# A three-stage attention kernel: its order of work taken from the framework's scheduler and written by a list schedule of its own

## The chip, the cores and the metric

The kernel runs on one core of a Trainium2 chip. The metric is the device time of one execution in microseconds. The core has a matmul engine (TensorE, PE in the rows, its weight loads PEld), VectorE (DVE), ScalarE (ACT), GpSimd (POOL), and SP, which only issues transfers here. Each engine works through its own instructions in order; the engines wait for each other by semaphores.

## The reference

Three stages follow each other on 4 batches of 544 positions (32 global and 512 local; 8 heads of 64, so 512 columns).

- Phase A, local and global attention: a local query sees the keys at a distance of at most 32 and the 32 global keys; a global query sees all 544. Softmax, then times v.
- Phase B, four experts of one head each: `logits = x @ w_gate`, the top two of four are kept with softmax weights; per expert `q = x @ wq[e]`, `k = x @ wk[e]`, `v = x @ wv[e]`, causal softmax attention, and `a @ v @ wo[e]`, summed with the gate weights.
- Phase C: `h = relu(x @ w_in)`, a convolution of three taps along the sequence, `h * sigmoid(conv) @ w_out`.

w_in, w_out and conv_w come as 64-bit floats, the others as 32-bit.

## The kernel before, in words

Work goes batch by batch through the phases; phase A takes a batch in four pairs of heads (16 pairs in all). Matmuls with accuracy to keep take each operand as a high and a low half (`split`, `sub`: L93 to L101) and issue three products for one.

A pair of phase A loads keys and queries (`raw`, L230, two buffers) and values (`vr`, L236, two buffers of 1 MB), makes the scores of the global queries (L244) and of the local ones (L261 adds the mask, L266 the scores), reduces to the maximum (L272), takes eight exps with their sums (L275), scales on POOL (L281), transposes (L296), and multiplies with v (L307; L320 for global queries) into `xh`, `xl`, of which there are five buffers (L217).

Phase B of a batch projects q and k (L378, 8 groups of 12 matmuls) and v with the gate (L391), computes the gate on VectorE, handles the last 32 rows apart (L438 and on), and goes through eight items (`scores`, `trans`, `pv`): score matmuls (L476), maximum, exp (L483) into two `w2` buffers, scaling on POOL (L490), transposes (L500), copies into two more `w2` buffers (L502), and times v (L512) into `oh`, `ol`. There are six `w2` buffers (L67); transfers of weights and the outputs take them too.

Phase C of a batch has two halves z. For each of eight f: six matmuls (L558), relu (L565 or L568), the middle tap (L570), two further taps on VectorE (L578, twice), tanh (L581), gating (L585), and a split into `gh`, `gl` (eight buffers each). `project` then runs through four m with 24 matmuls each (L598) and sends the result out (L603).

Two jobs are done once. The fold (`fold_gen`, L174) multiplies wo into w_in (L193), using `oh`, `ol` for its operand, so the first batch's `pv` comes after it. `wout_gen` (L208) prepares w_out. Both take 16 tiles of 64-bit floats through `load64` and `decode` (L103 to L116), six VectorE instructions and one of ScalarE, and one subtraction on POOL (L91).

The order is set in two steps. Three generators (phase A; projections and phase B; fold, w_out and phase C) yield estimated times, and `merge` (L628) takes the next piece from the one whose clock is lowest, at rates 60, 46 and 36, with flags for what must wait. That gives the program order. The framework's scheduler then orders each engine's instructions, with program order as priority and a timing model of its own; only groups in `paired()` keep their order on TensorE.

Of the kernel before, what the change touches and what calls it, by code (L numbers as in the profile page):

```python
# [8 lines left out]
F32 = mybir.dt.float32  # L9
# [24 lines left out]

def local_mask():

    import numpy as np
    m = np.zeros((128, 4, 128), np.float32)
    q = np.arange(32)[:, None]
    for n in range(NG_):  # L40
        for c, kb in enumerate(KEYS[FIRST[n]:FIRST[n] + 4]):
            if kb != "g":
                t = 32 * kb + np.arange(32)[None, :]
                ok = (abs(q + 32 * n - t) <= 32) & (t >= 0) & (t < SL)
                m[32 * (n % 4):32 * (n % 4) + 32, n // 4, 32 * c:32 * c + 32] = np.where(ok, 0.0, -BIG)
    return m


@with_exitstack
def body(ctx, tc, kq, vA, w_gate, wqk, wv, woT, w_in, conv_w, w_out, cmask, out):  # L50
    nc = tc.nc
    NB = kq.shape[0]
    pe, act, dve, pool, sp = nc.tensor, nc.scalar, nc.vector, nc.gpsimd, nc.sync
# [4 lines left out]
    def T(shape, dt, name, bufs=1):  # L58
        return sb.tile(shape, dt, name=name, bufs=bufs)

    def PS(*shape):
        return ps.tile([128] + list(shape), F32, name="s", bufs=5)

    def PO(*shape):
        return ps.tile([128] + list(shape), F32, name="t", bufs=3)

    NW = 6  # L67
# [14 lines left out]

    def paired():

        return tc.manual_schedule(engines={mybir.EngineType.PE})
# [17 lines left out]
    def decode(raw, w, dst=None):  # L103

        lo, up = raw[:, :, 0], raw[:, :, 1]
        t, f1, p, q = W1("hb", I32)[:, :w], W1("cv", I32)[:, :w], W1("hb", I32)[:, :w], W1("cv")[:, :w]
        dve.tensor_scalar(t, up, 3, 0x3FFFFFF8, op0=ALU.logical_shift_left, op1=ALU.bitwise_and)
        dve.scalar_tensor_tensor(f1, up, -0x40000000, t, op0=ALU.bitwise_and, op1=ALU.bitwise_or)
        dve.tensor_scalar(p, f1, -0x800000, None, op0=ALU.bitwise_and)
        dve.scalar_tensor_tensor(q, lo.bitcast(U32), 2.0 ** -52, p.bitcast(F32), op0=ALU.mult, op1=ALU.mult)  # L110
        dve.tensor_tensor(q, f1.bitcast(F32), q, op=ALU.add)

        e = W1("hb")[:, :w]
        act.activation(e, up.bitcast(F32), AF.Abs)
        dst = q if dst is None else dst
        dve.scalar_tensor_tensor(dst, e, GUARD, q, op0=ALU.is_ge, op1=ALU.mult)  # L116
# [9 lines left out]
    make_identity(nc, ident)  # L126
# [20 lines left out]
    flags = {"x_free": 0, "x_done": 0, "o_free": 0, "o_done": 0}  # L147

    def wait(flag, n):
        while flags[flag] < n:  # L150
            yield None

    def projections_gen():
        w = W2()
# [7 lines left out]
        for c in range(4):  # L162
            w = W2()
            sp.dma_start(w, wqk[128 * c:128 * c + 128])
            split(wqkh[:, c], wqkl[:, c], w, act)
            yield 3
        for c in range(4):
            w = W2()
# [3 lines left out]
            yield 3  # L172

    def fold_gen():  # L174

        woh = oh.rearrange("p a c -> p (a c)")[:, :1024].rearrange("p (c m) -> p c m", c=4)
        wol = ol.rearrange("p a c -> p (a c)")[:, :1024].rearrange("p (c m) -> p c m", c=4)
        for c in (0, 2):
# [3 lines left out]
        yield 1  # L182
        for n in range(4):
            accs = [PS(512) for _ in range(2)]
            for c in range(4):
                w = load64(w_in[128 * c:128 * c + 128, 256 * n:256 * n + 256])
# [3 lines left out]
                for m in range(2):  # L190
# [4 lines left out]
                yield 1.5  # L195
# [4 lines left out]
            yield 1  # L200
        flags["o_free"] = 2

    def conv_load():
        rawc = T([128, 24, 2], I32, "rawc")
# [3 lines left out]
    def wout_gen(n):  # L208
        for f in range(8):
            w = load64(w_out[128 * f:128 * f + 128, 256 * n:256 * n + 256])  # L210
# [3 lines left out]
            yield 2.5  # L214


    XB = 5  # L217
# [4 lines left out]
    Pg = T([64, 6, 128], F32, "Pg")  # L222
    pool.memset(Pg, 0.0)
# [9 lines left out]
    def load_v(n):  # L233

        vr = T([128, NG_, 128], F32, "vr", 2)
        sp.dma_start(vr, vA[n // 4, n % 4])  # L236
        return vr

    def scores_g(k, q):
# [3 lines left out]
        for z, kk in enumerate((k[:, 32:672].rearrange("p (m c) -> p m c", m=5)[:, :, 32:], k[:, 672:736])):  # L243
            pe.matmul(gt[z], q[:, SL:], kk, start=True, stop=True)  # L244
# [8 lines left out]
    def scores_l(k, q):  # L253
# [3 lines left out]
        with paired():  # L257
# [10 lines left out]
        yield 1.5  # L268
        ml = T([128, 2, 16], F32, "ml", 2)
        P = [T([128, 4, 128], F32, "Pa", 2) for _ in range(2)]  # L270
        for y in range(2):
# [5 lines left out]
            yield 0.5  # L277
# [6 lines left out]
    def trans_g():  # L284
        PGT = T([128, 6, 64], F32, "PGT")
        t = PO(6, 64)
        for m in range(6):
            pe.transpose(t[:, m, :], Pg[:, m], ident[:64, :64])
# [3 lines left out]
    def trans_l(P):  # L292
        PA = T([128, 4, 128], F32, "PA", 2)
        t = PO(4, 128)
        for i in range(4):
            pe.transpose(t[:, i, :], P[:, i], ident)  # L296
        act.activation(PA, t, AF.Copy)  # L297
        return PA

    def pv_l(vr, PA):  # L300

        o = PO(4, 128)
        with paired():
            for g in range(NG_):
                q = slice(32 * (g % 4), 32 * (g % 4) + 32)
                for y in range(2):
                    pe.matmul(o[64 * y:64 * y + 64, g // 4, q], vr[:, g, 64 * y:64 * y + 64], PA[y][:, g // 4, q],  # L307
# [3 lines left out]
    def pv_end(b, c, o, vr, PGT):  # L311
        xh, xl = xs[b, c] = T([128, S], F32R, "xh", XB), T([128, S], F32R, "xl", XB)
# [4 lines left out]
        with paired():  # L317
            for m, g in enumerate(PGW):
                for y in range(2):
                    pe.matmul(o[64 * y:64 * y + 64, :32], vr[:, g, 64 * y:64 * y + 64],  # L320
# [4 lines left out]
    def stream_a():  # L325

        NP = 4 * NB
        raw, vr = {}, {}
        for n in range(2):
            raw[n], vr[n] = load_kq(n), load_v(n)  # L330
# [3 lines left out]
        P = None  # L334
        for n in range(NP + 1):
            old, new = n >= 1, n < NP
            if old:
                PGT = trans_g()
                yield 0.3
                PA = [trans_l(P[y]) for y in range(2)]  # L340
                yield 0.9
            if new:
                scores_g(*raw[n])
                yield 0.8
            if old:
                b, c = divmod(n - 1, 4)
                yield from wait("x_free", b if c >= XB - 4 else b - 1)
                o = pv_l(vr[n - 1], PA)
                yield 1.0
            if new:  # L350
                P = yield from scores_l(*raw.pop(n))
                if n + 2 < NP:
                    raw[n + 2] = load_kq(n + 2)
            if old:
                pv_end(b, c, o, vr.pop(n - 1), PGT)
                yield 0.5
                if c == 3:
                    flags["x_done"] = b + 1
                if n + 1 < NP:
                    vr[n + 1] = load_v(n + 1)  # L360
# [3 lines left out]
    qll = T([128, 2, 128], F32R, "qlast_l")  # L364
    def phase_b(b):
        yield from wait("x_done", b + 1)
        xh, xl = zip(*[xs.pop((b, c)) for c in range(4)])
        qh, qlo, kh, kl = [T([128, 2, S], F32R, n) for n in ("qh", "qlo", "kh", "kl")]
        for t, (dh, dl, sc) in enumerate(((qh, qlo, 0.125), (kh, kl, 1.0))):
            for p in range(2):  # L370
                m = slice(256 * t + 128 * p, 256 * t + 128 * p + 128)
                for z in range(2):
# [3 lines left out]
                    for c in range(4):  # L376
# [4 lines left out]
                    yield 1.35  # L381
# [3 lines left out]
        for i in range(5):  # L385
# [3 lines left out]
            for c in range(4):  # L389
# [6 lines left out]
            yield 1.1  # L396
        flags["x_free"] = b + 1
# [26 lines left out]
        yield 0  # L424
# [8 lines left out]
        for z in range(2):  # L433
            t = PS(512)
            n = 0
            for p in range(2):
# [4 lines left out]
            if z:  # L441
# [11 lines left out]
        yield 1.5  # L453
        PLT = T([128, 5, 128], F32, "PLT")
        t = PO(4, 128)
        for j in range(4):
# [5 lines left out]
        yield 0.7  # L462
# [3 lines left out]
        def scores(p, i):  # L466
# [5 lines left out]
            with paired():  # L472
# [6 lines left out]
            PB = []  # L479
            for y in range(2):  # L480
                dve.tensor_reduce(st[:, y:y + 1], t[y][:, :w], axis=AX.X, op=ALU.max, negate=True)  # L481
                P = W2()
                act.activation(P[:, :w], t[y][:, :w], AF.Exp, bias=st[:, y:y + 1],  # L483
                               accum_out=st[:, 2 + y:3 + y])
                PB.append(P)
            yield 0.3 * (i + 1)
# [7 lines left out]
        def trans(p, i):  # L494
            PB = live[p, i]
            live[p, i] = []
            for y in range(2):
                t = PO(4, 128)
                for j in range(i + 1):
                    pe.transpose(t[:, j, :], PB[y][:, 128 * j:128 * j + 128], ident)  # L500
                PT = W2().rearrange("p (a b) -> p a b", a=4)
                dve.tensor_copy(PT[:, :i + 1], t[:, :i + 1])  # L502
                live[p, i].append(PT)
                yield 0.2 * (i + 1)

        def pv(p, i):
            PT = live.pop((p, i))
            o = PO(512)
            with paired():
# [4 lines left out]
            d = slice(128 * i, 128 * i + 128)  # L514
            act.activation(oh[:, p, d], o[:, :128], AF.Copy)
            sub(ol[:, p, d], o[:, :128], oh[:, p, d])
            yield 0.3 * (i + 1)
# [195 lines left out]
```

## Time and profile before

| what | value |
|---|---|
| median of 3 runs | 555.01 us (552.49 to 556.65) |
| the profiled execution | 555.79 us, its span 554.0 us |
| mean granted TensorE clock | 0.927 |
| PE, PEld, DVE, ACT, POOL busy | 503.8, 420.4, 356.2, 312.3, 131.7 us |
| HBM read and written | 38.66 MB and 4.46 MB |
| chain that ended last | PE 66%, DVE 17%, ACT 7%, DMA 5%, POOL 2%, issue 2% |

The span runs from the first instruction to the last. PE counts the time in which at least one matmul is running, with modelled ends; PEld that in which weights are loaded. The granted clock is the share of full speed (2.4 GHz) that TensorE was given.

### The profile page before, as it was taken

The page shows a single profiled execution, that of the slowest core. Times are in us where ns is not written, and L with a number is a line of the kernel's source. Part 1 is how long each engine was busy: PE and PEld are TensorE (multiplying, and loading weights), DVE is VectorE, ACT ScalarE, POOL GpSimd, SP SyncE. Part 2 cuts the span into 40 slices and gives each one's busy share as a digit, 9 for nine tenths or more (in the row PEclk, how much of TensorE's full clock was granted, in tenths as well). Part 3 has the DMA queues.
Part 4 walks back from the last instruction along what each step waited for, and adds up shares of the span by engine and source line. Part 5 has one row for each costly group of instructions (what it writes and reads, how often), then busy time and mean ns, then how long its engine had stood idle before and what let it go on. Part 6 is the DMA issues. An engine that isn't in the chain of part 4 may idle for free.

```text
span 554.0 us, 14597 instructions
## 1 busy us (share of the span) xinstructions
PE 503.8 (91%) x5688; PEld 420.4 (76%) x5688; DVE 356.2 (64%) x1059; ACT 312.3 (56%) x1048; POOL 131.7 (24%) x222
## 2 busy tenths in 40 slices
PE   3598798998987998999989999988999999999996
PEld 1266577995645687987667899976889998779996
DVE  1999976335557599975786429435694565694953
ACT  2657575434543567747786448246573663573764
POOL 2244452202242252224313300022221001231000
PEclk9787985997858799999999999979999999999999
DMA  8856622202324152013432200001000000000011
GB/s 336 256 156 215 224 95 102 77 1 89 128 96 147 69 173 77 1 52 109 137 123 72 83 21 1 12 20 69 11 12 32 11 2 21 10 12 11 31 41 43
DMA packets 16742, 44.06 MB, mean 80 GB/s; under 512 B 2592, under 2 KB 7840, under 8 KB 14624
## 3 DMA queue, kind: packets, MB, share of 16 engines
q1 hardware_dynamic: 16672, 43.12, 22.6%
q8 instruction: 45, 0.74, 0.6%
q14 instruction: 25, 0.20, 0.1%
HBM read 38.66 MB, written 4.46 MB: 78 GB/s over the span
## 4 chain that ended last, share of the span: by engine, by line
PE 66%; DVE 17%; ACT 7%; DMA 5%; POOL 2%; issue 2%; SPq 0%; ACTq 0%; POOLq 0%; DVEq 0%
PE s L598 18%; PE s L378 8%; PE s L558 7%; PE s L391 5%; PE t L512 3%; PE t L307 3%; ACT Pa L275 3%; PE s L476 3%; PE t L500 3%; PE s L266 3%; PE t L296 3%; DVE ml L272 2%; PE t L320 2%; DMA w<-in_woT_dram 2%; DVE cv L578 2%
## 5 line engine op out<-in xcount | busy, mean ns | idle before, releaser
L578 DVE SCALAR_TENSOR_TENSOR cv<-hb,cw,cv 128x272 f32<-128x272 f32 x128 | 65.8, 527 | 15.9 <-ACT cv L570 14.2
L598 PE MATMUL s<-gl,wuh 128*128 128x272 f32 x256 | 73.9, 296 | 0.0
L598 PE MATMUL s<-gh,wuh 128*128 128x272 f32 x256 | 71.2, 303 | 2.2 <-ACT w L483 1.9
L598 PE MATMUL s<-gh,wul 128*128 128x272 f32 x256 | 73.2, 294 | 0.0
L490 POOL TENSOR_SCALAR w<-w,stB,gate 128x128 f32<-128x128 f32 (+3 forms) x64 | 43.4, 688 | 91.3 <-DVE stB L488 64.3
L275 ACT ACTIVATE Pa<-s,ml 128x128 f32<-128x128 f32 x128 | 45.3, 376 | 15.7 <-DVE ml L273 13.9
L598 PEld LDWEIGHTS s<-gh,wuh 128*128 128x128 f32 x256 | 46.9, 193 | 4.7 <-ACT w L483 2.4
L598 PEld LDWEIGHTS s<-gl,wuh 128*128 128x128 f32 x256 | 49.2, 193 | 1.3 <-issue 1.1
L598 PEld LDWEIGHTS s<-gh,wul 128*128 128x128 f32 x256 | 48.9, 192 | 0.3
L281 POOL TENSOR_TENSOR Pa<-Pa,ml 128x512 f32<-128x512 f32 x32 | 33.6, 1070 | 39.3 <-DVE ml L279 28.5
L502 DVE COPY w<-t 128x128 f32<-128x128 f32 (+3 forms) x64 | 30.2, 485 | 19.8 <-PE t L500 19.5
L558 PE MATMUL s<-oh,wfh 128*128 128x274 f32 x128 | 39.8, 311 | 0.6 <-ACT hb L568 0.5
L378 PE MATMUL s<-xh,wqkh 128*128 128x272 f32 x128 | 38.5, 301 | 1.7 <-ACT hb L565 1.4
L307 PEld LDWEIGHTS t<-PA,vr 128*64 128x64 f32 x1024 | 35.2, 143 | 5.8 <-ACT PA L297 2.3
L307 PE MATMUL t<-PA,vr 128*64 128x32 f32 x1024 | 38.0, 228 | 1.5 <-ACT PA L297 1.5
L483 ACT ACTIVATE w<-s,stB 128x128 f32<-128x128 f32 (+3 forms) x64 | 33.4, 531 | 8.8 <-DVE stB L481 7.2
L378 PE MATMUL s<-xh,wqkl 128*128 128x272 f32 x128 | 37.7, 294 | 0.0
L378 PE MATMUL s<-xl,wqkh 128*128 128x272 f32 x128 | 37.4, 292 | 0.0
L558 PE MATMUL s<-ol,wfh 128*128 128x274 f32 x128 | 37.2, 291 | 0.0
L558 PE MATMUL s<-oh,wfl 128*128 128x274 f32 x128 | 37.2, 290 | 0.0
L581 ACT ACTIVATE cv<-cv 128x272 f32<-128x272 f32 x64 | 27.4, 429 | 12.7 <-DVE cv L578 12.4
L587 ACT ACTIVATE gh<-cv 128x272 fp32r<-128x272 f32 x64 | 27.4, 430 | 11.9 <-DVE cv L585 11.5
(158 smaller groups left out, 1357.3 us busy)
## 6 DMA issues: line engine op xcount, KB each, us to landing
vr<-in_vA_dram SPq DMA_DIRECT2D x16, 1024.0 KB, 5.1
raw<-in_kq_dram SPq DMA_DIRECT2D x16, 672.0 KB, 4.3
out_dram<-w SPq DMA_DIRECT2D x32, 136.0 KB, 1.8
w<-in_w_in_dram SPq DMA_DIRECT2D x16, 256.0 KB, 3.8
w<-in_w_out_dram SPq DMA_DIRECT2D x16, 256.0 KB, 3.3
w<-in_wqk_dram SPq DMA_DIRECT2D x4, 256.0 KB, 3.6
w<-in_woT_dram SPq DMA_DIRECT2D x2, 256.0 KB, 8.2
w<-in_wv_dram SPq DMA_DIRECT2D x4, 128.0 KB, 2.7
```

What stands on the lines that cost most here:

```text
L275: act.activation(P[y][:, i], t[y][:, i], AF.Exp, bias=ml[:, y, i:i + 1], scale=SCALE, accum_out=ml[:, y, 4 + i:5 + i])
L281: pool.tensor_tensor(P[y], P[y], ml[:, y, 12:16, None].to_broadcast([128, 4, 128]), op=ALU.mult)
L307: pe.matmul(o[64 * y:64 * y + 64, g // 4, q], vr[:, g, 64 * y:64 * y + 64], PA[y][:, g // 4, q], start=True, stop=True)
L378: pe.matmul(acc[:, :272], wa[:, c, m], xa[c][:, s], start=(n == 0), stop=(n == 11))
L391: pe.matmul(acc[:r, :260], xa[c][:, 128 * i:128 * i + r], wa[:, c, :], start=(n == 0), stop=(n == 11))
L483: act.activation(P[:, :w], t[y][:, :w], AF.Exp, bias=st[:, y:y + 1], accum_out=st[:, 2 + y:3 + y])
L490: pool.tensor_scalar(PB[y][:, :w], PB[y][:, :w], st[:, 4 + y:5 + y], gate[:, i, 2 * p + y:2 * p + y + 1], op0=ALU.mult, op1=ALU.mult)
L502: dve.tensor_copy(PT[:, :i + 1], t[:, :i + 1])
L558: pe.matmul(acc[:, :274], a[:, p, 128 * f:128 * f + 128], x[:, p, a0:a0 + 274], start=(k == 0), stop=(k == 5))
L578: dve.scalar_tensor_tensor(cv[:, :N], hb[:, o:o + N], cw[:, k, f:f + 1], cv[:, :N], op0=ALU.mult, op1=ALU.add)
L581: act.activation(cv[:, :N], cv[:, :N], AF.Tanh, scale=0.5)
L598: pe.matmul(acc[:, :N], w[:, f, sl], a, start=(f == 0 and k == 0), stop=(f == 7 and k == 2))
```

## The change

The three generators, the flags and `merge` go. All calls are recorded as nodes (an instruction, or a `group` of TensorE's that stays together), with tiles that have no memory yet; overlaps of what is read and written give the dependences. Each node has a due time, set by `due()`, and a cost by functions of the code. `schedule` runs a clock: at each event, for each engine that is free, it takes the ready node with the lowest due time whose new buffers are to be had. `engines` is in the order in which they first occur: DVE, POOL, SP, ACT, PE. A node that lacks a buffer marks that name as lacking for later nodes of the same event. Nodes that depend on nothing, all loads of weights among them, are ready from the start. `emit` writes the nodes in that order, with a manual schedule for every engine. `claim` takes a buffer for a tile at the group that precedes its first writer.

Buffers: `w2` five in place of six; `decode` has `d0`, `d1` (two each) in place of `hb`, `cv`; the transposed items have `PT` (two) and the outputs `y` (two) in place of `w2`; `xh`, `xl` four in place of five; `vr` three halves in place of two wholes, with two transfers to a pair.

The arithmetic is as before. The core of the diff:

```diff
+PERIOD, A_AT, A_STEP, LOAD_AHEAD = 60.0, 0.0, 10.0, 20.0
+B_AT, LAST, ITEMS, ITEM_STEP = 30.0, 34.0, 14.0, 2.5
+C_AT, C_HALF, C_PROJ = 75.0, 25.0, 12.0
+FOLD, FOLD_STEP, WOUT, WOUT_STEP = 30.0, 2.5, 75.0, 2.5
...
+    def schedule(self):
...
+            lacking = set()
+            for e in engines:
+                if free[e] > now + 1e-9:
+                    continue
+                for n in sorted(ready[e], key=lambda n: (n.due, n.seq)):
+                    if at[n] > now + 1e-9:
+                        continue
+                    need = {}
+                    for t in n.new:
+                        need[t.name] = need.get(t.name, 0) + 1
+                    short = [k for k, c in need.items() if used.get(k, 0) + c > [t.bufs for t in n.new if t.name == k][0]]
+                    if short or lacking & set(need):
+                        lacking |= set(short)
+                        continue
+                    ready[e].remove(n)
+                    for k, c in need.items():
+                        used[k] = used.get(k, 0) + c
+                    n.start = now
+                    if e.name == "SP":
+                        free[e] = now + 0.45
+                        dma = max(dma, now + 0.5) + n.cost
+                        n.end = dma + 1.6
+                    else:
+                        free[e] = n.end = now + n.cost
+                    order.append(n)
+                    heapq.heappush(times, free[e])
+                    for m in after.get(n, ()):
+                        at[m] = max(at[m], n.end + (0.02 if m.eng is e else n.lag))
+                        waits[m] -= 1
+                        if not waits[m]:
+                            ready[m.eng].append(m)
+                            heapq.heappush(times, at[m])
+                    for t in n.tiles:
+                        left[t] -= 1
+                        last[t] = max(last.get(t, 0.0), n.end)
+                        if not left[t]:
+                            back.append((last[t] + 0.1, t))
+                            heapq.heappush(times, last[t] + 0.1)
+                    break
+        return order
...
+    def emit(self, tc):
+        with tc.manual_schedule():
+            for n in self.schedule():
+                for method, args, kw in n.calls:
+                    real = lambda v: v.real() if isinstance(v, View) else v
+                    getattr(n.eng.nc, method)(*map(real, args), **{k: real(v) for k, v in kw.items()})
...
+def cost_pe(node, method, out, args, kw):
+    us = 0.0 if node.calls else 0.03
+    node.lag = 0.25
+    if method == "transpose":
+        return us + 0.11
+    lhs, N = args[1], width(out)
+    K, M = lhs.shape[0], width(lhs)
+    if lhs.dt == F32R:
+        one = max(0.107, N / 2400 + 0.013)
+        return us + (one if K > 64 else one / 2)
...
+def cost_act(node, method, out, args, kw):
+    return 0.18 + 0.0008 * width(out) + (0.19 if "accum_out" in kw else 0.0)
+def cost_dve(node, method, out, args, kw):
+    n = max(width(v) for v in list(args[:2]) + [out] if isinstance(v, View))
+    if n < 64:
+        return 0.17
+    return 0.15 + n * 0.00104 if method != "tensor_scalar" else 0.05 + n * 0.00104
+def cost_pool(node, method, out, args, kw):
+    n = width(out)
+    return 0.3 + n * 0.001 if method in ("tensor_scalar", "memset") else 0.3 + n * 0.002
...
-    NW = 6
+    NW = 5
...
-        t, f1, p, q = W1("hb", I32)[:, :w], W1("cv", I32)[:, :w], W1("hb", I32)[:, :w], W1("cv")[:, :w]
...
+        a, d = T([128, 256], F32, "d0", 2)[:, :w], T([128, 256], F32, "d1", 2)[:, :w]
+        ai, di = a.bitcast(I32), d.bitcast(I32)
+        dve.tensor_scalar(ai, up, 3, 0x3FFFFFF8, op0=ALU.logical_shift_left, op1=ALU.bitwise_and)
+        dve.scalar_tensor_tensor(di, up, -0x40000000, ai, op0=ALU.bitwise_and, op1=ALU.bitwise_or)
+        dve.tensor_scalar(ai, di, -0x800000, None, op0=ALU.bitwise_and)
+        dve.scalar_tensor_tensor(a, lo.bitcast(U32), 2.0 ** -52, a, op0=ALU.mult, op1=ALU.mult)
+        dve.tensor_tensor(d, d, a, op=ALU.add)
+        act.activation(a, up.bitcast(F32), AF.Abs)
...
-    XB = 5
+    XB = 4
+    NPA, NPT = 2, 2
...
+                due(FOLD + FOLD_STEP * (4 * n + c))
...
+            due(WOUT + WOUT_STEP * (8 * n + f))
...
+        at = B_AT + PERIOD * b
...
+                    due(at + 4 * t + 2 * p + z)
...
+            due(at + 8 + i)
...
-        vr = T([128, NG_, 128], F32, "vr", 2)
-        sp.dma_start(vr, vA[n // 4, n % 4])
+        vr = [T([128, NG_ // 2, 128], F32, "vr", 3) for _ in range(2)]
+        for h in range(2):
+            sp.dma_start(vr[h], vA[n // 4, n % 4][:, 8 * h:8 * h + 8])
...
+        P = [T([128, 4, 128], F32, "Pa", NPA) for _ in range(2)]
+        rec.claim(*P)
+        with rec.group():
...
+    def phase_a(b):
+        for c in range(4):
+            n = 4 * b + c
+            at = A_AT + PERIOD * b + A_STEP * c
+            due(at - LOAD_AHEAD)
+            kq_ = load_kq(n)
+            vr = load_v(n)
+            due(at)
+            scores_g(*kq_)
+            due(at + 1)
+            P = scores_l(*kq_)
+            due(at + A_STEP)
+            PGT = trans_g()
+            PA = [trans_l(P[y]) for y in range(2)]
+            due(at + A_STEP + 1)
+            o = pv_l(b, c, vr, PA)
+            pv_end(b, c, o, vr, PGT)
...
+            PB = [W2() for _ in range(2)]
+            rec.claim(*PB)
+            with rec.group():
...
+                PT = T([128, 4, 128], F32, "PT", NPT)
...
+        for n, (p, i) in enumerate(items):
+            due(at + ITEMS + ITEM_STEP * n)
+            scores(p, i)
+            due(at + ITEMS + ITEM_STEP * (n + 1))
+            trans(p, i)
+            due(at + ITEMS + ITEM_STEP * (n + 2))
+            pv(p, i)
+        due(at + ITEMS + ITEM_STEP * 10)
+        pv_last()
...
+                y = T([128, N], F32, "y", 2)
+                due(at + C_HALF * z + C_PROJ + 3 * m)
...
+            for f in range(8):
+                due(at + C_HALF * z + 1.2 * f)
+                s0(z, f)
+                s1(z, f)
+                s2(z, f)
+            project(z)
...
-    merge([stream_a(), stream_b(), stream_c()], [60, 46, 36])
+    consts_a()
+    projections_gen()
+    conv_load()
+    fold_gen()
+    for n in range(2):
+        wout_gen(n)
+    for b in range(NB):
+        phase_a(b)
+        phase_b(b)
+        phase_c(b)
+    rec.emit(tc)
```

## Rows read from the trace of the kernel before

**Rows 1.** The page, part 1: busy us, share of the span and instructions of each engine.

```profile
PE 503.8 (91%) x5688; PEld 420.4 (76%) x5688; DVE 356.2 (64%) x1059; ACT 312.3 (56%) x1048; POOL 131.7 (24%) x222
```

**Rows 2.** Chain of waits in order of time, last part: start us, us, what.

```profile
441.65 1.54 PE s L558 x12
...
537.40 11.30 PE s L598 x90
```

**Rows 3.** Single lines on TensorE: duration ns min/median/max, first and last start us.

```profile
L193 PE MATMUL s<-gl,oh x64: 276/283/583, 21.7 to 113.9; 128*128 128x256 f32 x64
...
L378 PE MATMUL s<-xh,wqkh x128: 282/288/594, 93.0 to 446.4; 128*128 128x272 f32 x128
...
L476 PE MATMUL s<-kh,qh x64: 323/437/792, 126.8 to 496.3; 64*128 64x128 f32 x16, 64*128 64x256 f32 x16, 64*128 64x384 f32 x16, 64*128 64x512 f32 x16
...
L558 PE MATMUL s<-oh,wfh x128: 283/291/399, 193.3 to 536.9; 128*128 128x274 f32 x128
```

**Rows 4.** Windows: length; busy (count) of PE, PEld, DVE, ACT, POOL; granted clock; DMA share, GB/s.

```profile
0.00:150.00 150.00, 121.01 (x1619) 91.84 (x1619) 97.52 (x298) 77.85 (x280) 44.97 (x58) 0.84 0.44 150
150.00:200.00 50.00, 43.25 (x510) 28.43 (x511) 30.68 (x92) 26.62 (x105) 17.29 (x20) 0.76 0.36 126
200.00:540.00 340.00, 330.14 (x3488) 290.88 (x3487) 222.44 (x658) 202.05 (x650) 69.38 (x144) 0.99 0.13 43
540.00:554.00 14.00, 9.44 (x76) 9.22 (x74) 5.57 (x15) 5.77 (x15) 0.10 (x1) 0.91 0.13 43
400.00:460.00 60.00, 60.00 (x535) 56.36 (x535) 38.15 (x101) 34.76 (x102) 6.05 (x21) 1.00 0.05 15
```

**Rows 5.** Groups by line and form, VectorE: busy us, mean ns, idle before and its releaser.

```profile
L107 DVE TENSOR_SCALAR hb<-w 128x256 int32<-128x256 int32 x32 | 10.2, 317 | 2.9 <-DMA w<-in_w_out_dram 2.9
...
L108 DVE SCALAR_TENSOR_TENSOR cv<-w,hb 128x256 int32<-128x256 int32 x32 | 15.2, 475 | 0.8 <-POOL gl L91 0.6
...
L109 DVE TENSOR_SCALAR hb<-cv 128x256 int32<-128x256 int32 x32 | 12.3, 384 | 0.3
...
L110 DVE SCALAR_TENSOR_TENSOR cv<-w,hb 128x256 f32<-128x256 uint32 x32 | 14.4, 449 | 2.3 <-POOL gl L91 0.9 <-POOL wul L91 0.6
...
L111 DVE TENSOR_TENSOR cv<-cv 128x256 f32<-128x256 f32 x32 | 15.0, 470 | 0.5
...
L116 DVE SCALAR_TENSOR_TENSOR cv<-hb,cv 128x256 f32<-128x256 f32 x32 | 17.1, 533 | 1.0 <-ACT PA L297 0.5
...
L272 DVE TENSOR_REDUCE ml<-s 128x4 f32<-128x512 f32 x32 | 20.6, 683 | 6.3 <-PE s L266 6.3
...
L245 DVE TENSOR_REDUCE mg<-s 64x1 f32<-64x480 f32 x16 | 10.3, 646 | 7.7 <-PE s L244 7.7
...
L101 DVE TENSOR_TENSOR xl<-t,xh 128x512 fp32r<-128x512 f32 x16 | 10.9, 681 | 4.5 <-ACT xh L314 4.3
...
L273 DVE TENSOR_SCALAR ml<-ml 128x4 f32<-128x4 f32 x32 | 5.3, 191 | 0.0
```

**Rows 6.** Line 116 on VectorE: duration ns min/median/max, first and last start us.

```profile
L116 DVE SCALAR_TENSOR_TENSOR cv<-hb,cv x32: 406/420/1045, 20.1 to 238.5; 128x256 f32<-128x256 f32 x32
```

**Rows 7.** Groups by line and form, evacuations on ACT and VectorE.

```profile
L275 ACT ACTIVATE Pa<-s,ml 128x128 f32<-128x128 f32 x128 | 45.3, 376 | 15.7 <-DVE ml L273 13.9 <-PE s L478 1.7
...
L275 ACT ACTIVATION_READ_ACCUMULATOR Pa<-s,ml 128x1 f32 x128 | 27.6, 216 | 0.0
...
L578 DVE SCALAR_TENSOR_TENSOR cv<-hb,cw,cv 128x272 f32<-128x272 f32 x128 | 65.8, 527 | 15.9 <-ACT cv L570 14.2 <-ACT oh L529 0.3 <-POOL hb L564 0.2
...
L570 ACT ACTIVATE cv<-hb,cw 128x272 f32<-128x272 f32 x64 | 33.1, 524 | 0.7
```

**Rows 8.** The page, part 6: DMA issues, KB each, median us to landing.

```profile
vr<-in_vA_dram SPq DMA_DIRECT2D x16, 1024.0 KB, 5.1
...
w<-in_w_out_dram SPq DMA_DIRECT2D x16, 256.0 KB, 3.3
```

**Rows 9.** Timeline of SP's queue at the start: start us, us, what.

```profile
1.15 0.42 SPq L236 DMA_DIRECT2D vr<-in_vA_dram  x1
```

More of the change, by code (lines that the diff above doesn't have):

```diff
@@ L49, in body, with cost_dma @@
+def cost_dma(node, method, out, args, kw):
+    v = out if isinstance(out, View) else args[1]
+    return v.shape[0] * width(v) * 4 / 300e3
 @with_exitstack
@@ L146, in body @@
     ol = T([128, 2, S], F32R, "ol")
[L147 to L151, printed above, removed]
     def projections_gen():
+        due(-5)
         w = W2()
@@ L222, in body @@
     Pg = T([64, 6, 128], F32, "Pg")
+    due(-5)
     pool.memset(Pg, 0.0)
@@ L286, in trans_g @@
         t = PO(6, 64)
-        for m in range(6):
-            pe.transpose(t[:, m, :], Pg[:, m], ident[:64, :64])
+        rec.claim(PGT)
+        with rec.group():
+            for m in range(6):
+                pe.transpose(t[:, m, :], Pg[:, m], ident[:64, :64])
         act.activation(PGT, t, AF.Copy)
@@ L323, in pv_end, with consts_a @@
         sub(xl[:, 0:32], o[:, :32], xh[:, 0:32])
[L325 to L330, printed above, removed]
+    def consts_a():
+        due(-15)
         w = W2()[:, :512]
@@ L388, in phase_b @@
             n = 0
-            for c in range(4):
+            due(at + 8 + i)
+            rec.claim(vB[:r, i], lg[:r, i])
+            with rec.group():
+              for c in range(4):
                 for xa, wa in ((xh, wvh), (xh, wvl), (xl, wvh)):
@@ L435, in phase_b @@
             n = 0
-            for p in range(2):
+            if z == 0:
+                rec.claim(PL)
+            with rec.group():
+              for p in range(2):
                 for a, k in ((ql, kh), (ql, kl), (qll, kh)):
@@ L555, in s0 @@
             a0, k = 270 * z, 0
-            for p in range(2):
+            hb, cv = W1("hb"), W1("cv")
+            rec.claim(hb, cv)
+            with rec.group():
+              for p in range(2):
                 for a, x in ((wfh, oh), (wfh, ol), (wfl, oh)):
@@ L628, in merge @@
-    def merge(streams, rates):
-        n = len(streams)
-        clock, live, stuck, late = [0.0] * n, set(range(n)), set(), set()
-        while live:
-            ready = live - stuck
-            i = min(ready, key=lambda i: clock[i])
-            y = next(streams[i], "end")
-            if y is None:
-                stuck.add(i)
-                late.add(i)
-                continue
-            if i in late:
-                late.remove(i)
-                clock[i] = max(clock[i], min([clock[j] for j in live - late - {i}] or [0.0]))
-            stuck.clear()
-            if y == "end":
-                live.remove(i)
-            else:
-                clock[i] += y / rates[i]
@@ L649, in body @@
-    merge([stream_a(), stream_b(), stream_c()], [60, 46, 36])
+                y = T([128, N], F32, "y", 2)
+                due(at + C_HALF * z + C_PROJ + 3 * m)
+                for f in range(0, 8, 2):
+                    if f == 0:
+                        rec.claim(y)
+                    with rec.group():
+                        for h in (f, f + 1):
+                            gh, gl = g[z, h]
+                            for k, (w, a) in enumerate(((wuh, gh), (wuh, gl), (wul, gh))):
+                                pe.matmul(acc[:, :N], w[:, h, sl], a, start=(h == 0 and k == 0), stop=(h == 7 and k == 2))
```

386 lines of the change are left out of this document (252 added, 134 removed).

## The prediction

> **What bounds the kernel now.** I read the page's first part, then the windows of the whole run, then the chain of waits, then single lines. TensorE looks almost full: 503.8 of 554.0 us busy [rows 1]. But a matmul's bar is 0.29 us long, while the chain shows 90 of them in 11.30 us, one per 0.126 us [rows 2, 3]. Bars overlap, and gaps of a bar's length vanish under them. The bars of the weight loads do not hide so much: 420.4 us [rows 1]. By the matmul bars the room would be 50 us, by the weight loads 134 us. The Trainium skill ("Perfetto Trace Analysis", Identifying the Most-Contended Engine) says the same in general: matmul busy time is no measure of distance from the roof, LDWEIGHTS busy time is. Without that sentence the count decides: the 1,536 matmuls of width 272 and 274 (768 on L598, 384 each on L378 and L558, by the loops) at 0.126 to 0.128 us make 194 us alone [rows 2], and in the fullest 60 us window weight loads fill 56.36 us [rows 4]. So I take 420 us as TensorE's work.
>
> Where are the other 134 us? Work done (weight-load time) by window [rows 4]: 91.8 of the first 150 us, 28.4 of the next 50, 290.9 of the 340 from 200 to 540, 9.2 of the last 14. Lost: 58, 22, 49 and 5. The first 200 us lose 80 of the 134, at a granted clock of 0.84 and 0.76, a mixture of the 1.2 and 2.4 GHz levels; from 200 on it is 0.99. Line by line [rows 3]: the fold of w_in ends at 113.9 us, batch 0's projections start at 93.0, its score items at 126.8, and the first matmul of phase C is at 193.3. The merge of three streams gives phase A of batches 0 and 1, the fold and then w_out's decoding turns, and phase C, which is the best filler there is (L598, L558: half of TensorE's big matmuls), is missing for 193 us.
>
> **The change part by part.** No arithmetic goes or comes: same matmuls, exps, splits, decodes. What moves is the order on every engine, and the buffers. I cost the pieces as stretches of the new run.
>
> *Start, up to batch 0's score items.* Due numbers put A(0) at 0 to 41, the fold at 30 to 70, B(0) at 30 to 69, A(1) at 60 to 101, w_out at 75 to 115. But the list schedule is greedy, and every weight load is ready from the start. SP comes ahead of TensorE in the loop over engines, so whenever one of the five w2 buffers comes free SP takes it for the next weight tile; B's score items claim two at once and find them only when the last of the 32 tiles is issued. I therefore expect that all decoding is done before B(0)'s items, which makes VectorE the bound: a decode is 317+475+384+449+470+533 ns = 2.63 us, 32 of them 84 us [rows 5]. A pair of phase A takes 2 x 0.683 + 0.646 + 0.681 and about nine small ones like L273's 0.191, in all 4.3 us; eight pairs 35 us [rows 5]. Some 26 splits of about 0.45 us (estimated from L101's and L116's rows) and small gate work add 17. Sum 136 us; with the first load (1 MB takes 5.1 us to land [rows 8]) and a nearly full VectorE, t = 150. Bounds: decoding that gives way to B(0) would bring its items to t = 75 (next part); a VectorE no fuller than in the first 150 us of before, 97.5 of 150 [rows 4], would take until 210. I take 150, because priority queues keep an engine with ready work full. By then TensorE has done the two phases A, the fold and the projections. Before had done the same kinds by 150, so I take its 91.8, less a little: 90.
>
> Here a rule speaks against the change. L116's decode step takes 420 ns in the median, 533 in the mean, 1045 at most [rows 5, 6], so something stops it at times. The Trainium skill ("SBUF — State Buffer", Who interferes with whom) says that a VectorE instruction with two SBUF inputs and a GpSimd one that reads SBUF exclude each other for the whole instruction. It fits sub_pool behind each decode; no row of before proves it. Priced by rows alone: if each of 32 decodes met one such stop of 0.62 us in place of the mean's 0.11, the start would end 16 us later, at 166. I take the mean, since w_in's decodes already ran this densely.
>
> *B(0)'s items alone.* Little stands beside them (phase A's pv waits for x, only four buffers now, until B(1) has projected, and B(1)'s projections need B(0)'s qh). I take the pace of before's 150 to 200, 0.57 [rows 4]: 17 us of work in 30, so 107 done at t = 180. Before stands at about 109 there. So far nothing is gained.
>
> *From 180 on.* 313 us of work are left. In before the rest ran at 0.57 until 200 and at 0.856 until 540 [rows 4]; phase C's first batch still had w_out's decoding beside it, whose last step starts at 238.5 [rows 6]. In the new order C(0), B(1) and A(2) are due together, no weight is left, and VectorE (356 us in all [rows 1], of which some 150 are spent) has about 206 for 340. I take 0.93, near the 0.939 of before's window 400 to 460 [rows 4]; bounds 0.856 and 0.97. 313 / 0.93 = 337, so t = 517; at 0.856 it is 366, t = 546; at 0.97, 323, t = 503.
>
> *Tail.* C(3) is due after all else, so VectorE's chain of a step (two L578 of 0.527, then more [rows 7]) stands bare for a while: 8 steps of about 2 us against 0.77 us of matmuls each (half of L558's 12 in 1.54 [rows 2]). Some 5 us more is my price (0 to 12).
>
> *Small edits, at nothing.* vr comes in halves: 16 more issues on SP, 0.42 us each [rows 9], on an engine that only issues; a 512 KB half should land between the 3.3 us of 256 KB and the 5.1 us of 1 MB [rows 8]. With three halves the next pair's second half waits for pv_end, and only phase A alone would feel that. Decode's own d0/d1, PT's two and y's two take work out of w2 and hb/cv; cover is that TensorE has other groups ready, and if it has none, the start price above already holds it. Claims at the matmul instead of at the eviction hold Pa, x and PB a microsecond or two earlier; the cover is the same.
>
> Sum: 150 + 30 + 337 + 5 = 522 us of span. The profiled execution was 555.79, 1.8 above its span, and 0.8 above the median: 523.
>
> **Rivals.** *The start is dense too* (chance 0.20): if B(0)'s items get their w2 before the decoding is done, the first part is only A(0), the fold and splits, 17 + 42 + 12 = 71 us of VectorE, t = 75 with some 40 us of TensorE work; then 380 / 0.94 = 404, tail 5, 486 with the 1.8. For it: A(0) goes ahead of the fold by due number. Against: SP's turn before TensorE's.
>
> *Nothing gained* (0.13): the start as above but ending at 166, and the later pace as before, 0.856: 166 + 30 + 366 = 562, less up to 10 where some of both is avoided: 552 to 562. Speaking for it: 5 and 3 PSUM buffers and two Pa are as before, and the dependences are the same.
>
> *Slower: TensorE waits in its fixed order* (0.19). The order is made from costs in the code, at full clock. An exp with its sum is 0.47 us there and 0.376 + 0.216 = 0.592 in the trace; a phase C step has 0.433 for L578 where the trace has 0.527, twice, and 0.398 for L570's 0.524 [rows 7]. A pair's eight exps come 1.0 us late, a C step's chain 0.3. If TensorE stands at each such place, with all groups of the other phases behind it in order: 16 x 1.0 + 32 x 0.25 + 64 x 0.35 = 46 us, on top of 523: 569. It decides when TensorE's losses go over the 134 us of now. Against it: the chip's own in-order queue already runs before on a modelled order, and many groups are not placed at their earliest moment.
>
> **How the numbers follow.** Forecast 0.48 (its own range 500 to 548), dense start 0.20, nothing gained 0.13, slower 0.19. The predicted time is the forecast's, 523. The range 482 to 566 reaches from the dense start to short of the full price of the slower rival, leaving about 0.06 below and 0.14 above. About 1% is what a measurement of this kernel tells from no change; under 549.5 us lie the forecast and the dense start, 0.68; within, 0.13; above 560.5, 0.19.
>
> **What would show it.** Right: weight-load time still about 420; first L476 near 150 and all decodes before it; first phase C matmul well before 193; after 180 a weight-load share of 0.93 at clock 1. Wrong: score items at 75 (dense start), w_out's decodes after phase C's start, a share of 0.86 later (nothing gained), or TensorE's waits for ACT and VectorE spread over many lines with a total of weight-load time plus more than 134 us of gaps (slower). A tail in which only L558 stands between long gaps would mean that I priced it too low.

## The result: faster by 3%, and the profile after

The changed kernel takes 538.02 us (median; 536.93 to 538.88) beside 555.83 of the kernel before: ratio 0.970, 95% interval 0.9645 to 0.9751. The forecast was 523 in a range of 482 to 566. The profiled execution's span is 536.7 us, against 554.0.

Part 1 of the page of the changed kernel, to be held against [rows 1]:

```profile
PE 480.3 (89%) x5688; PEld 408.2 (76%) x5688; DVE 372.1 (69%) x1059; ACT 316.6 (59%) x1048; POOL 127.5 (24%) x222
```

The number of instructions is the same; VectorE is busy 16 us longer, TensorE's bars are 23 us shorter. Windows of the changed kernel, columns as in [rows 4]:

```profile
0.00:160.00 160.00, 119.23 (x1799) 91.92 (x1799) 135.54 (x363) 89.49 (x322) 54.94 (x66) 0.84 0.54 179
160.00:180.00 20.00, 17.53 (x172) 10.55 (x170) 13.70 (x50) 10.77 (x44) 9.13 (x15) 0.75 0.10 36
180.00:520.00 340.00, 331.24 (x3647) 294.69 (x3646) 219.08 (x639) 211.81 (x674) 63.40 (x142) 0.99 0.12 41
520.00:536.70 16.70, 12.33 (x76) 11.03 (x74) 3.83 (x9) 4.50 (x12) 0.00 (x0) 0.90 0.10 34
...
0.00:200.00 200.00, 156.36 (x2146) 119.50 (x2146) 161.63 (x444) 111.91 (x409) 71.24 (x92) 0.85 0.44 147
200.00:536.70 336.70, 323.97 (x3544) 288.70 (x3542) 210.51 (x615) 204.67 (x639) 56.23 (x130) 0.99 0.13 43
```

By 200 us the weight loads stand at 119.5 us; before they stood at 91.84 + 28.43 = 120.3 [rows 4]. By this measure the start is no better, and the gain shows behind it: 336.7 us in place of 354.0. But weight loads last longer at a low clock (see the part on the prediction). Counted in TensorE's own work (an estimate, worked out below from TensorE alone), the changed kernel is 6 us ahead at 200 us, and the other 11 us of the gain come behind it. Single lines of the changed kernel, as in [rows 3, 6] (all instructions are emitted at L308, so tiles tell them apart): the first score maximum, the first matmul of phase C, the last step of a decode.

```profile
L308 DVE TENSOR_REDUCE stB<-s x64: 275/482/692, 160.4 to 476.1; 128x1 f32<-128x128 f32 x16, 128x1 f32<-128x256 f32 x16, 128x1 f32<-128x384 f32 x16, 128x1 f32<-128x512 f32 x16
...
L308 PE MATMUL s<-oh,wfh x128: 285/291/433, 203.4 to 519.1; 128*128 128x274 f32 x128
...
L308 DVE SCALAR_TENSOR_TENSOR d<-d,d x32: 365/421/1236, 37.6 to 161.9; 128x256 f32<-128x256 f32 x32
```

Batch 0's first score maximum comes at 160.4, 10 us later than forecast. All decoding but one last step (at 161.9) lies before it, as forecast. Phase C starts 10 us later than before, at 203.4 against 193.3.

### The profile page after: what moved, and what is told of

It reads as the page before. It is cut to its first block, busy times and chain, and to the rows that moved or that the text cites. A ratio compares the mean times of both kernels' runs of the same rounds, so it can differ in the third digit from the quotient of the medians.

```text
span 536.7 us, 14628 instructions
## 1 busy us (share of the span) xinstructions
PE 480.3 (89%) x5688; PEld 408.2 (76%) x5688; DVE 372.1 (69%) x1059; ACT 316.6 (59%) x1048; POOL 127.5 (24%) x222
## 4 chain that ended last, share of the span: by engine, by line
PE 55%; DVE 11%; ACT 5%; issue 2%; POOL 0%; DVEq 0%; ACTq 0%; POOLq 0%
PE s L308 41%; PE t L308 13%; DVE cv L308 5%; DVE d L308 1%; ACT cv L308 1%; DVE gl L308 1%; ACT hb L308 1%; DVE PT L308 1%; DVE ml L308 1%; DVE stB L308 1%; ACT Pa L308 1%; ACT gh L308 0%; ACT PA L308 0%; ACT w L308 0%; POOL w L308 0%
## 5 line engine op out<-in xcount | busy, mean ns | idle before, releaser
L308 PE MATMUL s<-gh,wuh 128*128 128x272 f32 x256 | 79.1, 309 | 2.7 <-ACT gh L308 2.7
L308 DVE SCALAR_TENSOR_TENSOR cv<-hb,cw,cv 128x272 f32<-128x272 f32 x128 | 65.6, 524 | 22.3 <-ACT cv L308 19.3
L308 PE MATMUL s<-gl,wuh 128*128 128x272 f32 x256 | 75.3, 294 | 2.9 <-DVE gl L308 2.5
L308 PE MATMUL s<-gh,wul 128*128 128x272 f32 x256 | 74.5, 291 | 0.0
L308 POOL TENSOR_SCALAR w<-w,stB,gate 128x128 f32<-128x128 f32 (+3 forms) x64 | 40.3, 639 | 132.5 <-DVE stB L308 49.5
L308 PE MATMUL s<-raw 64*32 64x128 f32 (+2 forms) x1088 | 46.9, 329 | 13.3 <-DMA raw<-in_kq_dram 6.9
L308 PEld LDWEIGHTS s<-gh,wuh 128*128 128x128 f32 x256 | 49.0, 191 | 6.4 <-ACT gh L308 3.8
L308 PEld LDWEIGHTS s<-gl,wuh 128*128 128x128 f32 x256 | 49.0, 191 | 5.0 <-DVE gl L308 5.0
L308 POOL TENSOR_TENSOR Pa<-Pa,ml 128x512 f32<-128x512 f32 x32 | 36.2, 1147 | 67.0 <-DVE ml L308 33.7
L308 PEld LDWEIGHTS s<-gh,wul 128*128 128x128 f32 x256 | 48.9, 191 | 0.0
L308 PEld LDWEIGHTS s<-raw 64*32 64x32 f32 (+1 forms) x1088 | 24.9, 125 | 30.8 <-issue 12.7
L308 ACT ACTIVATE w<-s,stB 128x128 f32<-128x128 f32 (+3 forms) x64 | 33.3, 525 | 24.7 <-DVE stB L308 21.1
L308 ACT ACTIVATE Pa<-s,ml 128x128 f32<-128x128 f32 x128 | 45.1, 374 | 0.7 <-DVE ml L308 0.7
L308 PE MATMUL s<-oh,wfh 128*128 128x274 f32 x128 | 39.9, 312 | 0.2 <-ACT hb L308 0.2
L308 DVE TENSOR_REDUCE stB<-s 128x1 f32<-128x128 f32 (+3 forms) x64 | 29.4, 484 | 12.6 <-PE s L308 12.5
L308 DVE COPY PT<-t 128x128 f32<-128x128 f32 (+3 forms) x64 | 29.9, 486 | 11.5 <-PE t L308 11.0
L308 PE MATMUL s<-ol,wfh 128*128 128x274 f32 x128 | 37.8, 295 | 0.0
L308 PE MATMUL s<-oh,wfl 128*128 128x274 f32 x128 | 37.7, 294 | 0.0
L308 PE MATMUL s<-xh,wqkh 128*128 128x272 f32 x128 | 37.7, 294 | 0.0
L308 PE MATMUL s<-xh,wqkl 128*128 128x272 f32 x128 | 36.9, 289 | 0.0
L308 PE MATMUL s<-xl,wqkh 128*128 128x272 f32 x128 | 36.8, 288 | 0.0
L308 ACT ACTIVATE cv<-cv 128x272 f32<-128x272 f32 x64 | 27.5, 430 | 15.3 <-DVE cv L308 14.4
```

What stands on the lines that cost most here:

```text
L308: getattr(n.eng.nc, method)(*map(real, args), **{k: real(v) for k, v in kw.items()})
```

## The experiments

Theory at the outset: the order of the list gives the gain and the buffers none. Rival: the buffers give it. Times are medians, ratios against runs of the kernel before on the same chip, with 95% intervals.

**The order as a priority only.** The manual schedule is taken off all but TensorE's groups:

```diff
-        with tc.manual_schedule():
-            for n in self.schedule():
+        from contextlib import nullcontext
+        for n in self.schedule():
+            pair = len(n.calls) > 1
+            with tc.manual_schedule(engines={mybir.EngineType.PE}) if pair else nullcontext():
```

> Same recorded order and same buffers, but the order is only the priority: the framework's scheduler again orders each engine, and only TensorE's groups keep their order inside. If the gain comes from the list's order and its buffers, 538 us give or take 5. If it comes from holding every engine to a fixed order, the gain goes: 550 to 556.

564.8 us, ratio 1.014 (1.007 to 1.020), above both forecasts. Left to the framework's scheduler, this order is 1% slower than the streams. Holding the engines to it is worth 27 us (538.0 against 564.8, on two chips).

**The buffers without the order.** The kernel before with `w2` five, own `d0`, `d1`, `PT`, `y`, four `xh`, `xl`, and `vr` in halves:

> The old three streams and the framework's scheduler with all the new buffers (w2 five, own d0/d1, PT and y, xh and xl four, vr in halves with two transfers). If the buffers carry the gain: 538 to 545. If the order carries it: 550 to 560, the old time.

533.5 us, 0.959 (0.949 to 0.968). The buffers alone give at least as much as the whole change (0.970; the intervals overlap). The first theory falls. The new order on the old buffers was not run, so what it would give there stays open. The parts of the buffers, each in the kernel before:

> The kernel before with d0 and d1 alone for the decode (and x in four buffers, to make room). Theory D: decodes and phase C's steps no longer share hb and cv, so phase C starts earlier (first TensorE matmul of phase C at 171 to 180 instead of 193) and the time is 533 to 541. Theory P, that PT's own buffers carry the gain: 551 to 558.

> The kernel before with own buffers for the transposed items (PT) and the outputs (y), w2 five and x four. Theory P: B's items no longer share w2 with the loads of weights, time 533 to 541. Theory D, that the decode's buffers carry the gain: 550 to 558.

> The kernel before with the values loaded in halves into three half buffers, with two transfers to a pair, and nothing else. Neither theory gives it a part in the gain: 552 to 560. Slower past 562 would say that the third half costs phase A something.

> The kernel before with two own buffers for the transposed items (PT) alone; the outputs stay in w2, which keeps six, and x has four. If PT carries the gain of its run with y: 535 to 543, item stretches of about 58 us in place of 72 for batch 0. If the outputs' hold on w2 until their transfer carries it: 550 to 557.

| in the kernel before | median us | ratio (95%) | batch 0's items, us |
|---|---|---|---|
| decode's d0, d1; x four | 555.9 | 1.000 (0.997 to 1.003) | not read |
| PT and y; w2 five; x four | 538.8 | 0.970 (0.963 to 0.977) | 58 |
| vr in halves | 552.1 | 0.995 (0.991 to 1.000) | not read |
| PT alone; w2 six; x four | 530.4 | 0.954 (0.947 to 0.961) | 56 |

The last column is the stretch in which VectorE works on batch 0's `stB`, read in windows of 2 us; before it is 72. The window of the kernel before and that of the last row (length, VectorE's work on `stB`, clock, DMA share, GB/s):

```profile
128.00:200.00 72.00, 11.07 (x32) 0.76 0.34 119
...
114.00:170.00 56.00, 11.27 (x32) 0.88 0.43 148
```

The whole of the last edit:

```diff
-    XB = 5
+    XB = 4
-                PT = W2().rearrange("p (a b) -> p a b", a=4)
+                PT = T([128, 4, 128], F32, "PT", 2)
```

Four `xh`, together with `d0` and `d1` (first row), change nothing, so PT does it: two buffers of its own for the transposed items, with six `w2` left. In the run of the first row phase C starts 16 us sooner than before, as theory D said, and the time still does not move; an early phase C alone is not what pays:

```profile
L558 PE MATMUL s<-oh,wfh x128: 285/292/595, 177.6 to 535.9; 128*128 128x274 f32 x128
```

Moving the outputs out as well and cutting `w2` to five takes 8 us of it back; which of the two does was not separated. Windows of the kernel with PT alone:

```profile
0.00:200.00 200.00, 165.85 (x2241) 129.65 (x2242) 154.70 (x452) 115.35 (x416) 69.39 (x91) 0.94 0.43 146
200.00:527.20 327.20, 318.92 (x3450) 278.98 (x3448) 203.08 (x609) 193.51 (x634) 63.83 (x131) 0.99 0.13 45
```

It wins on both sides of 200 us: 129.7 us of weight loads by then for 120.3, the clock 0.94 for 0.82, and 327.2 us for the rest. By the estimate below, 19 of its 27 us are won by 200 us.

SP's rows show one thing that the shared buffers did. In the kernel before, the loads of 64-bit weights into `w2` (L121) wait for L512, the matmul that reads the transposed items, and the last one is issued at 212.6 (SP's waits: total us, times, longest; then the loads of w_out):

```profile
SPq L121 <- DVE cv L110: 20.5, 9, 4.0
...
SPq L121 <- PE t L512: 8.3, 2, 5.7
...
L121 SPq DMA_DIRECT2D w<-in_w_out_dram x16: 327/328/967, 55.4 to 212.6; - x16
```

With PT alone no load waits for L512, and the last one is issued at 182.1:

```profile
L121 SPq DMA_DIRECT2D w<-in_w_out_dram x16: 327/328/423, 56.3 to 182.1; - x16
```

**The start.** Two tests of the claim on `w2` and of VectorE as the bound. First, `NW = 3` and `raw = T([128, 512], F32, "ld", 2).bitcast(I32)` in `load64`:

> The changed kernel with w2 cut to three and two buffers of their own for the 32 decoded tiles, so that batch 0's score items no longer wait for w2 until the last weight tile is issued. Both theories: the first score maximum on VectorE moves from 160 us to 80 or 90. My theory (VectorE bounds the start, so the work is only exchanged): total 530 to 545. Rival, the dense start: 495 to 510.

562.7 us, 1.011 (1.002 to 1.019). The claim holds, the items come at 88.4, as the row shows, but the time is worse than either forecast.

```profile
L308 DVE TENSOR_REDUCE stB<-s x64: 250/486/692, 88.4 to 499.9; 128x1 f32<-128x128 f32 x16, 128x1 f32<-128x256 f32 x16, 128x1 f32<-128x384 f32 x16, 128x1 f32<-128x512 f32 x16
...
PE t L308 <- POOL w L308: 9.6, 11, 1.7
PE s L308 <- DMA raw<-in_kq_dram: 8.6, 3, 4.8
PE s L308 <- ACT w L308: 7.4, 11, 1.5
```

TensorE now waits for the items' exps and scalings (line, total us, times, longest): `w2` of three holds one item and a half, and batch 0's items drag on for 72 us. So two things were changed at once, and the run says nothing for or against an early start as such.

Second, three of a decode's steps (L109, L110, L111 of before) left out:

> The changed kernel with three of the six VectorE steps of each decode left out (the decoded weights are then wrong), some 1.3 us less for each of 32 tiles, 42 us less of VectorE. If VectorE bounds the start: first score maximum at about 118 instead of 160 us and the total at 500 to 512. Rival (latencies and buffers hold the start): first score maximum past 145, total 530 or more.

534.1 us, 0.958 (0.951 to 0.964); the first score maximum at 142.2:

```profile
L308 DVE TENSOR_REDUCE stB<-s x64: 281/486/692, 142.2 to 471.9; 128x1 f32<-128x128 f32 x16, 128x1 f32<-128x256 f32 x16, 128x1 f32<-128x384 f32 x16, 128x1 f32<-128x512 f32 x16
```

VectorE is busy 36 us less (335.7 for 372.1; 42 were expected). Of these 18 us reach the items, between both forecasts, and 4 us the end, where the time is the rival's. VectorE shares the start, it does not set it alone.

**GpSimd beside the decodes.** `sub_pool` of both weights replaced by a copy on ScalarE:

> The changed kernel with the 32 GpSimd subtractions behind the decodes left out (the low half of the decoded weights is a scaled copy by ScalarE, so its values are wrong). If GpSimd stops VectorE, a decode's six steps fall from 3.0 us to 2.5 or less and the first score maximum comes some 12 us sooner, near 148. If not, they stay near 3.0 us and the first score maximum near 160.

One run, 533.6 us. Groups of the changed kernel and, below, of this one (mean ns before the bar):

```profile
L308 DVE TENSOR_SCALAR d<-w 128x256 int32<-128x256 int32 x32 | 19.5, 618 | 1.8 <-DMA w<-in_w_in_dram 1.6
L308 DVE SCALAR_TENSOR_TENSOR d<-w,d 128x256 int32<-128x256 int32 x32 | 18.5, 579 | 0.6 <-POOL gl L308 0.3
```

```profile
L308 DVE SCALAR_TENSOR_TENSOR d<-w,d 128x256 int32<-128x256 int32 x32 | 15.0, 470 | 3.0 <-ACT gl L308 2.1 <-ACT wul L308 0.6
L308 DVE TENSOR_SCALAR d<-w 128x256 int32<-128x256 int32 x32 | 11.9, 378 | 1.7 <-DMA w<-in_w_in_dram 1.7
```

All six steps sum to 3.00 us in the changed kernel, 2.64 here, 2.63 before [rows 5]. The first score maximum comes 7 us sooner, at 153.3; but the list is made anew for this kernel and ScalarE has 9 us more to do, so the 7 us need not be the subtractions' alone. GpSimd's work does lengthen VectorE's, as the Trainium skill ("SBUF — State Buffer", Who interferes with whom) has it for steps with two SBUF inputs and GpSimd instructions that read SBUF; here the step with one input is lengthened most. The changed kernel's trace shows it directly: 130 of the 192 decode steps overlap no GpSimd instruction, and none of these takes more than 427 ns; all longer ones, up to 1614 ns, run beside one. Without the subtractions the worst step still takes 1.26 us; it runs beside GpSimd's scaling of phase A's `Pa`.

**TensorE alone.** Only the matmul groups are emitted, in the changed kernel's order:

> All TensorE groups of the changed kernel in their order, with nothing of the other engines between them: operands are filled once from an input, nothing is evicted, so the result is not the reference's. From its first to its last matmul it measures TensorE's work without waits. The prediction took 420 us from the weight loads. Counting matmuls by the pace of dense stretches gives about 436. A value over 480 would mean that the later pace of 0.87 is not waiting but TensorE's own work.

One run, 449.4 us. Its page and its first matmul of phase C:

```profile
PE 440.5 (98%) x5688; PEld 387.8 (87%) x5688; ACT 40.0 (9%) x90; POOL 0.7 (0%) x6
...
L334 PE MATMUL s<-oh,wfh x128: 283/290/398, 136.8 to 436.5; 128*128 128x274 f32 x128
```

TensorE's work is 441 us (first matmul at 6.0, span 447.6, clock 1.0), and weight loads fill only 387.8 / 440.5 = 0.88 of it though nothing waits. The order being the same, positions can be compared: phase C begins after 136.8 - 6.0 = 131 us of work, which takes the changed kernel 203 us, and the 311 us behind it take 333. It loses 72 us ahead of phase C and 22 after.

The run also gives an estimate of the work done by a moment in any of the kernels: each matmul counts with the mean time from its start to the next start that its shape takes here. By 180 us that is 106 us in the kernel before and 107 in the changed one; by 200 us it is 120, 126, and 139 with PT alone. From 180 to 480 us the changed kernel does 292 us of work in 300, the kernel before 267. The changed kernel's last 57 us hold 42 us of work, so 14 are lost there; before, the last 74 lose 6. The windows of the changed kernel and, below, of the kernel before:

```profile
180.00:480.00 300.00, 295.58 (x3364) 261.88 (x3362) 193.28 (x576) 185.84 (x604) 60.13 (x124) 1.00 0.13 45
480.00:536.70 56.70, 47.98 (x358) 43.85 (x357) 29.64 (x72) 30.48 (x81) 3.26 (x19) 0.94 0.06 21
```

```profile
180.00:480.00 300.00, 289.19 (x3226) 249.38 (x3226) 191.70 (x587) 174.61 (x582) 66.94 (x123) 0.98 0.15 52
480.00:554.00 74.00, 69.27 (x576) 64.36 (x574) 49.54 (x124) 45.48 (x127) 9.43 (x29) 0.98 0.08 26
```

**Other due times, and the same buffers under the old streams.** The second is the control of the first:

```diff
-PERIOD, A_AT, A_STEP, LOAD_AHEAD = 60.0, 0.0, 10.0, 20.0
+PERIOD, A_AT, A_STEP, LOAD_AHEAD = 45.36, 0.0, 13.11, 23.05
-B_AT, LAST, ITEMS, ITEM_STEP = 30.0, 34.0, 14.0, 2.5
+B_AT, LAST, ITEMS, ITEM_STEP = 37.5, 30.38, 12.29, 2.5
-C_AT, C_HALF, C_PROJ = 75.0, 25.0, 12.0
+C_AT, C_HALF, C_PROJ = 66.83, 30.94, 13.23
-FOLD, FOLD_STEP, WOUT, WOUT_STEP = 30.0, 2.5, 75.0, 2.5
+FOLD, FOLD_STEP, WOUT, WOUT_STEP = 27.0, 2.49, 71.95, 2.24
...
```

(also `w2` four, `ld` two, `hb` and `cv` four, `vr` two halves, and 1.88 in place of 1.2 between the f)

> The changed kernel with other due times (batches every 45 in place of 60, B at 37.5, C at 66.8 with halves 31 apart) and buffers shared out otherwise: w2 four and two of their own for decoded loads, hb and cv four, vr two halves. If the list schedule can pay with due times that fit, 505 to 525. If a fixed order cannot beat the streams whatever the due times, 533 or more.

> The old streams and the framework's scheduler with the same sharing out of buffers as the run with other due times. If buffers are what pays there, its time is within 8 us of that run. If the due times pay, this one is 15 us or more behind it, at 528 to 545.

506.0 us, 0.909 (0.901 to 0.918), and 538.5 us, 0.969 (0.962 to 0.976). On these buffers the list schedule with these due times beats the streams by 32 us, and it is the fastest version here. Under the streams these buffers are no better than the change's (538.5 against 533.5); how much of the way from 538 to 506 they and how much the due times have under the list was not separated. The windows of the 506 us run and its first score maximum:

```profile
0.00:200.00 200.00, 168.02 (x2265) 136.83 (x2266) 168.25 (x480) 125.41 (x437) 69.18 (x96) 0.93 0.44 143
200.00:505.30 305.30, 297.40 (x3425) 263.00 (x3424) 192.59 (x581) 188.09 (x611) 60.83 (x126) 1.00 0.16 51
...
L308 DVE TENSOR_REDUCE stB<-s x64: 269/483/693, 103.0 to 450.6; 128x1 f32<-128x128 f32 x16, 128x1 f32<-128x256 f32 x16, 128x1 f32<-128x384 f32 x16, 128x1 f32<-128x512 f32 x16
```

Behind 200 us its share of weight loads is 263.0 / 305.3 = 0.861, the changed kernel's 288.7 / 336.7 = 0.857. Most of the advantage, 31 us of span, is in the start: 136.8 for 119.5 us by 200, the items at 103 and not 160. By the estimate above 22 us are won by 200 us and some 9 behind it, which the share of weight loads does not show.

## Why the prediction was right, and where it was not

The sign and half of the size came true, 18 us where 32 were forecast, and the time lies in the forecast's own range of 500 to 548. The way there was another, and luck has a part in it. Of the signs named for "right", decoding before the items came (their first score matmul, L476 of before, at 156.8 and not 150), and weight-load time, 408.2, is still about 420. But phase C's first matmul came later and not well before 193, and the share of weight loads after 180 is 0.86 to 0.87, near the 0.86 that was named for "nothing gained". TensorE had more work than forecast and did it faster up to 480 us; these errors offset each other in part. Step by step:

- **TensorE's work, 420 us: mis-sized.** It is 441. The prediction took weight loads for work, on the Trainium skill ("Perfetto Trace Analysis", Identifying the Most-Contended Engine) as well as on [rows 1, 4]. Weight loads do not fill the time even when nothing waits (0.88), and they grow at a low clock (420.4 in the kernel before at 0.927, 387.8 at full clock). In the kernel before, those of L500 take 212 ns in the mean from 176.2 to 186.3 us, at a granted clock of 0.50 (1.2 GHz), and 140 from 400 to 460, at 1.00 (2.4 GHz; the two rows below the list). Here the matmul bars (440.5) were the better measure of the run without waits, though not of the gaps in the others.
- **The start to 150, VectorE as the bound:** right in place, 160 measured, with VectorE busy 135.5 of those 160. That this equals the 136 us priced is partly chance: the decodes alone took 32 x 0.37 = 12 us more than priced, and durations added up are more than the time taken, because bars overlap (a step of 0.43 us at 149.63 is followed by one at 149.98). The 16 us, priced for a rule and set aside, were thus nearer than the mean; but 0.30 of the 0.37 us stand in the first step (618 for 317 ns), which has one SBUF input and is not among those that the rule was quoted for. Of the 10 us too many, up to 7 are the subtractions' (without them 153.3). That VectorE alone sets it was wrong (light decode). (In the prediction's sum a pair of phase A adds up to 4.4 us and not 4.3; the 35 for eight is right.) The claim about `w2` was right; the reason given, SP's turn before TensorE's, was not tested.
- **Items alone, 30 us at 0.57:** 10.55 of 20 us, 0.53, and no lead over before at 180 us (107 against 106 us of work by the estimate): right.
- **From 180 on, 0.93:** as a share of weight loads it is 294.69 / 340 = 0.867 up to 520, and TensorE alone has 0.88. The window 400 to 460 [rows 4], from which 0.939 was read, has many projections, whose weight loads are dense, and does not stand for the mix. In work by the estimate it is 292 / 300 = 0.97 up to 480, where before had 267 / 300 = 0.89: better than forecast. From phase C's start to the end it is 311 / 333 = 0.93; that this agrees with the forecast is chance, since it includes the tail.
- **Tail, 5 us: mis-sized.** By the estimate 14 us are lost behind 480, above the upper bound of 12; TensorE's longest waits there are for `gh` and `gl`, the operands that ScalarE and VectorE make for `project`.
- **Small edits at nothing: the step that failed.** That "cover is that TensorE has other groups ready" was wrong for PT (right for d0 and d1, 1.000, and nearly for vr's halves, 0.995). Its two buffers give 25 us in the kernel before, more than the change as a whole. What was forecast of the order can be had from the buffers alone. Against the streams with the same buffers the order with its due times gains nothing (538.0 against 533.5 on another chip's runs; by ratios 0.970 against 0.959, whose intervals overlap).
- **Rivals.** "Slower in its fixed order" falls for this list: fixed, it is 27 us faster than free. "The start is dense too" did not happen, but the run with other due times goes that way: items at 103 us, 506 in place of the rival's 486. "Nothing gained" did not happen, though the share that was to show it came: a share of weight loads does not tell it from the forecast.

```profile
L500 PEld LDWEIGHTS t<-ident,w 128*128 128x128 f32 x6 | 1.0, 212 | 1.5 <-POOL w L490 1.1 <-issue 0.4
...
L500 PEld LDWEIGHTS t<-ident,w 128*128 128x128 f32 x25 | 2.9, 140 | 0.0
```

Where PT helps is shown by the shorter stretch of items (56 us for 72) and by the weight loads, which no longer wait for L512 and end 30 us sooner. That these two make up the whole 25 us is not shown. That the framework's scheduler had also put the shortage of buffers into its order is argued, not shown.

## What to carry to other kernels

When a change moves the order and the buffers together, try each alone: here one private pair of buffers, in the old kernel, was worth more than the whole change, and the order paid only with other due times and buffers to go with them. Measure an engine's work by running it alone before pricing its gaps by a busy share. Due times are a schedule's input, not its result: the same scheduler gave 538 us, or 506 with other due times and buffers.

## What was not expected of the hardware

A VectorE step of one SBUF input (decode's first, 289 ns in the median) took 618 ns in the mean with GpSimd's subtractions in the kernel and 378 without them. The halves of `vr`, sent in pairs, took 5.3 us each to land in the median, no less than the 5.1 of a whole [rows 8]; between 3.3 and 5.1 was forecast.

```profile
vr<-in_vA_dram SPq DMA_DIRECT2D x32, 512.0 KB, 5.3
```
